# Silu as one activation, and weight loads issued apart from their conversion, in a gated-attention kernel with a feed-forward block

## The chip, the cores and the metric

The kernel runs on one core of one Trainium2 chip. The metric is the device time of one execution in microseconds (us); lower is better. A profile is one traced execution, whose span is a little shorter than the time. The engines are PE (TensorE, matrix products), PEld (its weight loads), DVE (VectorE), ACT (ScalarE), POOL (GpSimd) and SP (SyncE, here only an issuer of DMAs). The granted clock is the share of PE's full clock that the profile's records show.

Unless a range is given, times are medians. The executions of one kernel spread over 0.4 to 4.7 us (the kernel before over 7.1 us in eleven executions), so a difference under 2 us between two times is not resolved; where one matters, I read it from the traces. The experiments ran on two chips, on which the kernel before took much the same (medians of 736.81 and of 737.04 to 737.39), and each ratio is to the kernel before in the same rounds.

## The reference, cut to what matters

```python
# attention: a complex-valued decaying state per head, over 768 steps
mag = np.sqrt(a_re*a_re + a_im*a_im)
scale = np.minimum(mag, 0.999) / (mag + 1e-06)
...
S_re, S_im = ar*S_re - ai*S_im + kv, ar*S_im + ai*S_re
y[:, :, t] = einsum(q[:, :, t], S_re)
# feed-forward on the 3072 rows of y
h = x @ w_in                    # 384 -> 2048
g = h * (1.0 / (1.0 + np.exp(-h)))   # silu
return g @ w_out                # 2048 -> 384
```

Everything is float32 inside the kernel; the weights come as float64 and are converted on the chip by integer operations on DVE.

## The kernel before

The 768 steps are cut into chunks of 128; with 4 batches that makes 24 chunks, handled as 12 pairs. A pair goes through these stages:

1. gates: logarithm, exponential and arctangent on ACT, a phase sum on PE, sines on ACT;
2. rotation of k and q on DVE, transposition into `T` (on PE for early chunks; on DVE and by DMA for later ones);
3. attention scores `a`, state `s`, output `y` on PE, and a copy to `xT`;
4. hidden products `h` on PE, `g = silu(h)`, output products `o` on PE.

The hidden layer of one pair is interleaved with the attention of the next. The activation of a hidden group was made of two operations:

```python
def hidden(p, jp):
    ...                                     # 12 matmuls into ps: h, 128 x 512
    g = moe.tile([C, 2, T], F32, tag="g", name=f"g{p}_{jp}", bufs=4)
    special(g, ps, AF.Tanh, scale=0.5)                    # ACT
    with tc.high_priority():
        nc.vector.scalar_tensor_tensor(out=g, in0=g, scalar=1.0, in1=ps,
                                       op0=ALU.add, op1=ALU.mult)   # DVE
# and at the end of a pair: nc.scalar.mul(out=ot, in_=..., mul=0.5)
```

From the fourth pair on every engine's order is written by hand. One step reads (h and r are hidden and output groups on PE, A and B the two chunks of the pair):

```python
usual = ("c h h E kA qA L F h kB h tA G r qB r h tB r th h A X r h r aA pA sA yA h pB aB S r lA "
         "sB yB r lB D r")
# E: exp table, decays   L, F: logarithms, inverse   kA, qA: rotation   tA: transposes for T
# G: ratio, arctangent   aA: scores
```

Before that only PE's order is fixed; the other engines' order is chosen when the program is built. The start:

```python
load_a(0)                      # gate inputs of the first pair, by SP
load_a(1, g)                   # of the second pair, by POOL (g = nc.gpsimd)
gates(0, True)                 # squares, then the exp table, logarithms, ...
table("trig"); gates_atan(0, True); gates_square(1); gates_angle(0, True)
both(phases, 0); both(sums, 0); turns(0)
gates_log(1); gates_inverse(1); gates_ratio(1)
convert(3)                     # each: fetch a block of weights, then convert it
...                            # k, q, v of the first pair, by SP
```

## Time and profile before

| what | us |
|---|---|
| time, median (range of 4 runs) | 738.94 (737.51 to 739.36) |
| span of the profile | 737.3 |
| PE busy, DVE busy, ACT busy | 678.7, 392.2, 352.2 |
| first matmul (phases of the first pair) | 22.88 |
| first hidden matmul | 70.58 |
| first scores of the second hand-ordered step, where the regular steps begin | 287.91 |
| six steps from there | 332.50 (55.4 each) |

PE is nearly always busy after the first hidden matmul. So the table is read as a relay: how late PE gets its first real work, how long it takes from there to the regular part, and how long a regular step lasts. An engine's busy total says little by itself. The lines of the profile stand in the prediction below.

### The profile page before, as it was taken

Reading aid. Unit: us, or ns where it says so; the run is one execution under the profiler, and the core shown is the slowest. Engines: PE = TensorE matmul, PEld = TensorE weight load, DVE = VectorE, ACT = ScalarE, POOL = GpSimd, SP = SyncE. Lnnn points to the kernel's source line nnn. Section 1 sums busy time; section 2 is a strip of 40 time slices with the busy share of each in tenths; the row PEclk is TensorE's granted clock in tenths of the full one; section 3 lists DMA queues with packets and bytes.
Section 4 is the critical chain, followed back from the end, with each engine's and each line's share of the span. In section 5 each row is a group of like instructions: output and inputs, shape, how many; then the busy total and the mean of one; then the engine's idle time right before and its main releaser. Section 6 shows DMA issues by size and latency. Waiting matters only on the chain.

```text
span 737.3 us, 9570 instructions
## 1 busy us (share of the span) xinstructions
PE 678.7 (92%) x3552; PEld 513.2 (70%) x3552; DVE 392.2 (53%) x638; ACT 352.2 (48%) x589; POOL 72.1 (10%) x111
## 2 busy tenths in 40 slices
PE   0465999899999999999999999999999999999997
PEld 0154877568667777777777777777777777778774
DVE  3878889835463348348348348348348347262110
ACT  6987569367572461461461461461461461331201
POOL 2355021030110010010010010010010010010000
PEclk9986999999999999999999999999999999999999
DMA  9494654010160005605605604605605605414000
GB/s 188 112 233 123 159 146 144 22 43 2 49 108 1 20 8 79 138 6 85 125 12 79 132 10 76 134 13 81 128 12 79 131 11 80 99 19 68 29 1 25
DMA packets 205894, 55.52 MB, mean 75 GB/s; under 512 B 196376, under 2 KB 200624, under 8 KB 205840
## 3 DMA queue, kind: packets, MB, share of 16 engines
q1 hardware_dynamic: 198096, 43.05, 30.3%
q0 software_dynamic: 4288, 7.06, 4.6%
q10 hardware_dynamic: 3456, 4.72, 1.7%
q8 instruction: 30, 0.49, 0.3%
q14 instruction: 24, 0.20, 0.1%
HBM read 36.25 MB, written 4.76 MB: 56 GB/s over the span
## 4 chain that ended last, share of the span: by engine, by line
PE 64%; ACT 11%; DVE 9%; SPq 5%; issue 5%; DMA 4%; POOL 1%; DVEq 0%; ACTq 0%; POOLq 0%
PE o L472 23%; PE h L457 22%; PE a L390 5%; SPq L382 5%; PE s L439 4%; PE y L411 3%; ACT s L227 3%; ACT mag L227 2%; PE y L414 2%; PE L L327 2%; ACT L222 2%; DMA raw<-in_moe_w_in_dram 2%; DVE g L462 2%; PE phase L306 2%; DMA T<-sq 1%
## 5 line engine op out<-in xcount | busy, mean ns | idle before, releaser
L457 PE MATMUL h<-xT,w 128*128 128x256 f32 x1152 | 261.7, 382 | 7.9 <-DMA decs<-ends 7.9
L472 PE MATMUL o<-w,g 128*128 128x384 f32 x768 | 262.8, 490 | 0.0
L457 PEld LDWEIGHTS h<-xT,w 128*128 128x128 f32 x1152 | 219.6, 192 | 49.7 <-ACT x L181 8.1
L472 PEld LDWEIGHTS o<-w,g 128*128 128x128 f32 x768 | 145.0, 191 | 89.8 <-issue 3.7
L462 DVE SCALAR_TENSOR_TENSOR g<-g,h 128x512 f32<-128x512 f32 x96 | 65.1, 683 | 202.0 <-ACT g L227 201.8
L227 ACT ACTIVATE g<-h 128x512 f32<-128x512 f32 x96 | 55.3, 594 | 153.8 <-PE h L457 153.6
L341 POOL DMA_DIRECT2D decs<-ends x48 | 30.1, 634 | 443.8 <-DMA ends<-eq 443.5
L420 ACT COPY xT<-y 128x384 f32<-128x384 f32 x24 | 11.5, 478 | 120.0 <-PE y L414 109.4
L390 PEld LDWEIGHTS a<-T 96*128 96x128 f32 x384 | 46.4, 194 | 14.1 <-issue 8.4
L390 PE MATMUL a<-T 96*128 96x128 f32 x384 | 48.3, 279 | 5.2 <-DMA T<-sq 3.0
L222 ACT ACT_TABLE_LOAD x41 | 52.6, 1283 | 0.7
L227 ACT ACTIVATE mag<-mag 128x768 f32<-128x768 f32 (+1 forms) x39 | 30.5, 788 | 44.9 <-DVE mag L272 44.5
L306 PE MATMUL phase<-th,upto 128*128 128x384 f32 x48 | 21.5, 549 | 25.6 <-DVE th L285 25.2
L330 DVE TENSOR_SCALAR L<-L 128x384 f32<-128x384 f32 x24 | 13.3, 556 | 54.6 <-PE L L327 54.6
L395 DVE TENSOR_TENSOR w<-a,upto 128x512 f32<-128x512 f32 x48 | 32.0, 684 | 18.2 <-PE a L390 18.2
L411 PE MATMUL y<-w,v 128*64 128x128 f32 (+1 forms) x384 | 39.6, 281 | 0.0
L414 PE MATMUL y<-T,S 96*64 96x128 f32 x320 | 34.2, 273 | 0.0
L439 PEld LDWEIGHTS s<-v,kr 128*96 128x96 f32 x320 | 29.9, 165 | 5.8 <-issue 2.2
L478 ACT ACTIVATE ot<-o 128x384 f32<-128x384 f32 x24 | 11.8, 490 | 40.3 <-PE o L472 40.3
L439 PE MATMUL s<-v,kr 128*96 128x48 f32 x320 | 30.0, 247 | 0.9 <-DVE w L395 0.8
L227 ACT ACTIVATE s<-s 128x768 f32<-128x768 f32 (+1 forms) x39 | 30.5, 784 | 0.3
L306 PEld LDWEIGHTS phase<-th,upto 128*128 128x128 f32 x48 | 9.0, 207 | 28.6 <-issue 26.3
(71 smaller groups left out, 648.4 us busy)
## 6 DMA issues: line engine op xcount, KB each, us to landing
T<-sq SPq DMA_DIRECT2D x192, 64.0 KB
raw<-in_moe_w_out_dram SPq DMA_DIRECT2D x16, 384.0 KB
raw<-in_moe_w_in_dram SPq DMA_DIRECT2D x24, 192.0 KB
out_dram<-ot ACTq DMA_DIRECT2D x24, 192.0 KB
k<-in_k_dram SPq DMA_DIRECT2D x18, 192.0 KB
q<-in_q_dram SPq DMA_DIRECT2D x18, 192.0 KB
v<-in_v_dram SPq DMA_DIRECT2D x18, 192.0 KB
re<-in_a_re_dram SPq DMA_DIRECT2D x16, 192.0 KB
```

The lines of the kernel that those rows point to most:

```text
L222: chain(nc.scalar.preload_act_table_set({"exp": "natural_log_exp_and_others", "trig": "trig_and_small", "atan": "sigmoid_and_others", "sin ...
L227: chain(nc.scalar.activation(out=out, in_=in_, func=func, **kw))
L306: nc.tensor.matmul(ps, lhsT=upto, rhs=th, start=True, stop=True)
L382: nc.sync.dma_start(out=to[ts(b, Q), :, a], in_=sq[ts(a, Q), b])
L390: nc.tensor.matmul(ps[:, h], lhsT=x["kT"][:, hh * HH + h], rhs=x["qT"][:, hh * HH + h], start=True, stop=True)
L395: nc.vector.tensor_tensor(out=x["w", hh], in0=ps, in1=upto.unsqueeze(1).to_broadcast([C, HH, C]), op=ALU.mult)
L411: nc.tensor.matmul(to, lhsT=v_[:, cols], rhs=x["w", h // HH][:, h % HH], start=True, stop=not carried)
L414: nc.tensor.matmul(to, lhsT=x["S"].rearrange("p h d -> p (h d)")[:, cols], rhs=x["qT"][:, h], start=False, stop=True)
L439: nc.tensor.matmul(ps[:, h], lhsT=x["kr"][:, h].rearrange("p c d -> p (c d)"), rhs=x["v"][:, h], start=True, stop=True)
L457: nc.tensor.matmul(ps[:, ji], lhsT=w1[:, dc, ts(jp * 2 + ji, C)], rhs=A[p]["xT"][:, dc], start=(dc == 0), stop=(dc == ND - 1))
L462: nc.vector.scalar_tensor_tensor(out=g, in0=g, scalar=1.0, in1=ps, op0=ALU.add, op1=ALU.mult)
L472: nc.tensor.matmul(A[p]["o"][m], lhsT=A[p]["g", jp][:, ji, ts(m, C)], rhs=w2[:, j], start=(j == 0), stop=(j == NJ - 1))
```

## The change

Silu becomes one ACT function, which frees DVE of 96 operations. Tanh and the arctangent ran from one table set; the kernel runs silu and the arctangent from two, so the arctangent now has a table load on each side; the separate load for the sines goes. The fetch of a weight block is split from its conversion, so that fetches can be issued early and in a chosen order with the gate inputs. The first table is loaded before the first inputs are there. The early transfers of `xT` go from POOL to SP.

```diff
-        special(g, ps, AF.Tanh, scale=0.5)
-        with tc.high_priority():
-            nc.vector.scalar_tensor_tensor(out=g, in0=g, scalar=1.0, in1=ps, op0=ALU.add,
-                                           op1=ALU.mult)
+        special(g, ps, AF.Silu)
...
-                nc.scalar.mul(out=ot, in_=A[p]["o"][m], mul=0.5)
+                nc.scalar.copy(out=ot, in_=A[p]["o"][m])
...
-            what["S"] = lambda: (table("sin"), both(trig, p + 1))
+            what["S"] = lambda: both(trig, p + 1)
-            what["F"] = lambda: (gates_inverse(p + 1), table("atan"))
-            what["G"] = lambda: (gates_ratio(p + 1), gates_atan(p + 1))
+            what["F"] = lambda: (gates_inverse(p + 1), table("silu"))
+            what["G"] = lambda: (gates_ratio(p + 1), table("trig"), gates_atan(p + 1),
+                                 table("silu"))
...                                   (the same for the early pairs)
-                (nc.sync if late else nc.gpsimd).dma_start(      # xT
+                nc.sync.dma_start(
...
-        load_a(1, g)
-        gates(0, True)
+        load_a(0)                     # one piece now on ACT's queue
+        fetch(2)
+        load_a(1)
+        fetch(1)
+        both(lambda n: load_x(n, "k"), 0)
+        both(lambda n: load_x(n, "q"), 0)
+        fetch(1)
+        both(lambda n: load_x(n, "v", g), 0)
+        table("exp")
+        gates_square(0, True)
...
```

Cut: the splitting of `load_w` into `fetch` and `convert` with four raw buffers in place of five, a sixth gate buffer, and the removal of pools that nothing used.

More of the change, by code (lines that the diff above doesn't have):

```diff
@@ L94 @@
     LB = 2
+    RAW = 4
     consts = ctx.enter_context(tc.tile_pool(name="consts", bufs=1))
@@ L133, in load_a @@
             for name, ap in (("re", a_re), ("im", a_im)):
-                (queue or nc.sync).dma_start(
+                (queue or (nc.scalar if p + i == 0 and name == "im" else nc.sync)).dma_start(
                     out=cut(A[p][name], i).rearrange("p (h d) -> p h d", d=D),
@@ L146, in load_x @@
                 out=X[n][name], in_=ap[b].rearrange("h (c p) d -> p c h d", p=C)[:, c])
-    units = []
     tiny = consts.tile([C, ND * (DF // WC) + NJ], F32)
@@ L152 @@
     w2 = consts.tile([C, NJ, DM], F32)
-    def load_w1(cols, dc):
-        load_w(w1[:, dc, ts(cols, WC)],
-               [(at, w_in[r:r + n, ts(cols, WC)]) for at, r, n in rows_in(H, D, ND, dc)])
-    def load_w2(j):
-        load_w(w2[:, j], [(0, w_out[ts(j, C)])])
-    def load_w(dst, parts):
-        n = dst.shape[1]
-        if parts[0][1].dtype == F32:
-            for at, src in parts:
-                nc.sync.dma_start(out=dst[at:at + src.shape[0]], in_=src)
-            return
-        raw = su.tile([C, WC, 2], I32, tag="raw", name="raw", bufs=5)[:, 0:n]
-        for at, src in parts:
-            nc.sync.dma_start(out=raw[at:at + src.shape[0]],
-                              in_=src.bitcast(I32).rearrange("p (n two) -> p n two", two=2))
-        lo, hi = raw[:, :, 0].bitcast(U32), raw[:, :, 1]
-        u = su.tile([C, WC], I32, tag="wu", name="u", bufs=2)[:, 0:n]
-        joined(nc, dst, lo, hi, u)
-        x = su.tile([C, WC], F32, tag="wx", name="x", bufs=1)[:, 0:n]
-        nc.scalar.activation(out=x, in_=hi.bitcast(F32), func=AF.Square, scale=2.0 ** 15)
-        nc.scalar.activation(out=x, in_=x, func=AF.Relu, scale=-1.0, bias=least_b,
-                             accum_out=tiny[:, ds(len(units), 1)])
-        units.append(dst)
@@ new lines, with fetch @@
+    blocks = []
+    for s in range(DF // WC):
+        for dc in range(ND):
+            blocks.append((w1[:, dc, ts(s, WC)], (1, s), [
+                (at, w_in[r:r + n, ts(s, WC)]) for at, r, n in rows_in(H, D, ND, dc)]))
+        for j in range(s * WC // C, (s + 1) * WC // C):
+            blocks.append((w2[:, j], (2, j // 2), [(0, w_out[ts(j, C)])]))
+    fetched, done = [], []
+    def fetch(n):
+        for dst, _, parts in blocks[len(fetched):len(fetched) + n]:
+            raw = su.tile([C, WC, 2], I32, tag="raw", name="raw", bufs=RAW)[:, 0:dst.shape[1]]
+            for at, src in parts:
+                if src.dtype == F32:
+                    nc.sync.dma_start(out=dst[at:at + src.shape[0]], in_=src)
+                else:
+                    nc.sync.dma_start(
+                        out=raw[at:at + src.shape[0]],
+                        in_=src.bitcast(I32).rearrange("p (n two) -> p n two", two=2))
+            fetched.append(raw)
@@ new lines, in convert @@
+    def convert(n):
+        for dst, _, parts in blocks[len(done):len(done) + n]:
+            if len(done) == len(fetched):
+                fetch(1)
+            raw = fetched[len(done)]
+            done.append(dst)
+            if parts[0][1].dtype == F32:
+                continue
+            lo, hi = raw[:, :, 0].bitcast(U32), raw[:, :, 1]
+            u = su.tile([C, WC], I32, tag="wu", name="u", bufs=2)[:, 0:dst.shape[1]]
+            joined(nc, dst, lo, hi, u)
+            x = su.tile([C, WC], F32, tag="wx", name="x", bufs=1)[:, 0:dst.shape[1]]
+            nc.scalar.activation(out=x, in_=hi.bitcast(F32), func=AF.Square, scale=2.0 ** 15)
+            nc.scalar.activation(out=x, in_=x, func=AF.Relu, scale=-1.0, bias=least_b,
+                                 accum_out=tiny[:, ds(len(done) - 1, 1)])
@@ L187, in keep, with converted @@
+    def converted(which):
+        while any(x[1] == which for x in blocks[len(done):]):
+            convert(1)
     def keep(t, pattern, base, mult, fill=0.0):
@@ L222, in table @@
         chain(nc.scalar.preload_act_table_set({
-            "exp": "natural_log_exp_and_others", "trig": "trig_and_small", "atan": "sigmoid_and_others",
-            "sin": "silu_and_others"}[of]))
+            "exp": "natural_log_exp_and_others", "trig": "trig_and_small",
+            "silu": "silu_and_others"}[of]))
     def special(out, in_, func, **kw):
@@ L240, in gates_square @@
         for x in ("s1", "s2", "mag"):
-            g[x] = flat(pre.tile([C, 2, H, D], F32, tag="t3", name=f"{x}{p}", bufs=5))
+            g[x] = flat(pre.tile([C, 2, H, D], F32, tag="t3", name=f"{x}{p}", bufs=6))
         for x in ("l", "th"):
@@ L316, in trig @@
         x = X[n]
-        x["cs"] = pre.tile([C, H, 2, D], F32, tag="t3", name=f"cs{n}", bufs=5)
+        x["cs"] = pre.tile([C, H, 2, D], F32, tag="t3", name=f"cs{n}", bufs=6)
         special(x["cs"][:, :, 1], heads(x["turn"]), AF.Sin, scale=TWO_PI)
@@ L427, in output @@
             for dc in range(ND):
-                (nc.sync if late else nc.gpsimd).dma_start(
+                nc.sync.dma_start(
                     out=xT[64 * r + D:64 * r + 64, dc],
@@ L512, in step @@
         else:
-            what["F"] = lambda: table("atan")
+            what["F"] = lambda: table("silu")
         if p + 2 < NP:
@@ L523, in part @@
             if f is hidden:
-                converted(1, jp // 2)
+                converted((1, jp // 2))
             else:
-                converted(2, jp)
+                converted((2, jp))
             f(p, jp)
@@ L535, in parts @@
         return take
-    load_a(0)
-    conv = []
-    for s in range(4):
-        conv += [(1, s, lambda s=s, dc=dc: load_w1(s, dc)) for dc in range(ND)]
-        conv += [(2, j // 2, lambda j=j: load_w2(j)) for j in range(4 * s, 4 * s + 4)]
-    def converted(which, i):
-        while any(x[:2] == (which, i) for x in conv):
-            conv.pop(0)[2]()
-    def convert(n):
-        for _ in range(n):
-            if conv:
-                conv.pop(0)[2]()
     def attend(n):
@@ L589 @@
     with tc.manual_schedule(engines={mybir.EngineType.PE}):
-        load_a(1, g)
-        gates(0, True)
+        load_a(0)
[4 more added lines that the diff above has]
+        both(lambda n: load_x(n, "q"), 0)
+        fetch(1)
+        both(lambda n: load_x(n, "v", g), 0)
+        table("exp")
+        gates_square(0, True)
+        gates_log(0, True)
+        gates_inverse(0, True)
+        gates_ratio(0, True)
         table("trig")
@@ L602 @@
         convert(3)
-        both(lambda n: load_x(n, "k"), 0)
-        both(lambda n: load_x(n, "q"), 0)
-        both(lambda n: load_x(n, "v"), 0)
         for n in (0, 1):
@@ L616 @@
         turns(1)
-        table("sin")
+        table("silu")
         for n in (2, 3):
@@ L632 @@
         gates(2)
-        table("atan")
+        table("silu")
         convert(7)
         groups("r0 r0 r1 r1 h1 h1")
+        table("trig")
         angles(2)
+        table("silu")
         groups("h0 h0")
@@ L642 @@
         groups("r1 r1 h1 h1")
-        table("sin")
         turns(2)
-        table("sin")
+        table("silu")
         for n in (4, 5):
@@ L655 @@
         attend(5)
-        table("atan")
+        table("trig")
         angles(3)
+        table("silu")
         groups("r0 r0 r1 r1")
@@ L661 @@
         load_a(4, g)
-        table("sin")
         both(trig, 3)
@@ L666 @@
         late.append(fast.enter_context(tc.tile_pool(name="late", bufs=1)))
-        late.append(fast.enter_context(tc.tile_pool(name="o_late", bufs=2, space=PSUM)))
-        late.append(fast.enter_context(tc.tile_pool(name="h_late", bufs=1, space=PSUM)))
-        late.append(fast.enter_context(tc.tile_pool(name="m_late", bufs=1, space=PSUM)))
         late.append(fast.enter_context(tc.tile_pool(name="o_late", bufs=2, space=PSUM)))
```

## The prediction

> **What bounds the kernel now.** I read the page first: its busy shares and slices, then the stretches, then the tensor engine's own timeline with the idle time ahead of each group, and last ACT and DVE in the two places where that timeline shows idle time.
>
> ```profile
> PE 678.7 (92%) x3552; PEld 513.2 (70%) x3552; DVE 392.2 (53%) x638; ACT 352.2 (48%) x589; POOL 72.1 (10%) x111
> PE   0465999899999999999999999999999999999997
> PEclk9986999999999999999999999999999999999999
> ```
>
> PE is busy 92% of the span, and its idle time lies in the first four slices (74 us). The clock is low only in the third and fourth.
>
> ```profile
> 60.00:80.00 20.00, 12.00 (x73) 10.40 (x74) 16.47 (x32) 12.33 (x27) 10.14 (x15) 0.74 0.48 137
> 80.00:100.00 20.00, 19.56 (x146) 16.18 (x145) 18.40 (x39) 8.67 (x20) 5.06 (x8) 1.00 0.65 165
> 311.60:367.40 55.80, 54.75 (x297) 41.87 (x297) 29.28 (x43) 24.25 (x38) 2.50 (x4) 1.00 0.40 73
> ```
>
> The columns are stretch and length, then busy time of PE, weight loads, DVE, ACT and POOL, granted clock, DMA share, GB/s. From 80 us on PE is full. In a repeated step of some 55 us DVE is busy 29 and ACT 24: relieving them buys nothing by itself. So the time is (start of the first hidden-layer matmul) + (a nearly solid PE queue), plus a few gaps.
>
> ```profile
> 22.88 2.90 PE L306 MATMUL phase<-th,upto 128*128 128x384 f32 x4 [22.88 <-DVE th L285]
> 51.17 2.68 PE L306 MATMUL phase<-th,upto 128*128 128x384 f32 x4 [2.36 <-DVE th L285]
> 61.63 1.09 PE L411 MATMUL y<-w,v 128*64 128x128 f32 x16
> 70.58 7.75 PE L457 MATMUL h<-xT,w 128*128 128x256 f32 x24 [7.86 <-DMA decs<-ends]
> ...
> 343.68 2.02 PE L390 MATMUL a<-T 96*128 96x128 f32 x16 [1.05 <-DMA T<-sq]
> ```
>
> The first matmul waits 22.9 us for the first pair's angles; the dense part starts at 70.58, after the transposed attention result xT has been moved. Later the only recurring gap is before the attention scores: 0.42, 1.05, 0.37, 0.52, 0.18, 0.37, 0.62 and 0.84 us over the steps, together 4.4.
>
> The front is an ACT chain:
>
> ```profile
> 7.08 0.52 ACT L227 ACTIVATE s<-re 128x384 f32<-128x384 f32 x1 [1.52 <-DMA re<-in_a_re_dram]
> 8.87 0.52 ACT L227 ACTIVATE s<-im 128x384 f32<-128x384 f32 x1 [1.27 <-DMA im<-in_a_im_dram]
> 9.30 0.51 ACT L227 ACTIVATE th<-re 128x384 f32<-128x384 f32 x1
> 9.83 1.28 ACT L222 ACT_TABLE_LOAD   x1
> 11.12 0.52 ACT L227 ACTIVATE s<-s 128x384 f32<-128x384 f32 x1
> ```
>
> ACT waits for gate inputs until 8.87, loads a table on the path, and only then takes logarithms. From 12 to 24 us it is busy 11.75 of 12.
>
> **What the Trainium skill says.**
> 1. "ScalarE: Activation LUTs", What ACT_TABLE_LOAD costs: a load takes about 1283 ns whatever the set. The trace agrees (41 loads, mean 1283). It adds about 1380 ns of drain; here the function after a load starts at once (9.83+1.28, next at 11.12), so I count 1.28.
> 2. Same page, What happens when an `exp` ACTIVATE runs: one element per cycle per lane for every function. The trace holds tanh of 128x512 at 594 ns; so I take silu at 594 too. No run has shown silu yet.
> 3. "DMA: Bandwidth & Descriptors", Queues, rings and completion order: each DMA engine takes turns between queues at packet granularity. In the trace the second pair's loads, issued by POOL from 1.78 us, are in flight with the first pair's on SP; the first pair's last piece, issued at 2.80, reached ACT only at 8.87, six us later, against 2.9 for its first piece (0.82 to 3.69).
> 4. "TensorE: Matmul & The Clock Gate", Part 1: the clock is halved when PE has been idle and comes back after sustained work. The trace agrees: the first 24 hidden matmuls took 7.75 us at 70.58, later ones 5.34.
>
> **The change part by part.**
>
> *Silu for tanh and a product.* 96 DVE operations of 683 ns go: 65.1 us, so DVE busy should fall to about 327. ACT keeps 96 operations of the same length; the final scaling becomes a copy of the same length. Table loads: silu and arctangent do not share a set, so the arctangent now has a load before and one after. I count the calls: before 14 early and 27 in the steps, and one set by the compiler, 42; after 15 early, and in the steps 9 exp, 10 silu and 8 pairs around the arctangent, 35: in all 50. Eight more are 10.3 us of ACT work, busy about 362.
>
> What is on the path? In a step DVE stands behind the product of g:
>
> ```profile
> 267.63 0.95 DVE L263 TENSOR_TENSOR mag<-mag,th 128x768 f32<-128x768 f32 x1
> 273.37 0.69 DVE L462 SCALAR_TENSOR_TENSOR g<-g,h 128x512 f32<-128x512 f32 x1 [4.79 <-ACT g L227]
> 273.98 0.55 DVE L350 TENSOR_TENSOR L<-k,L 128x384 f32<-128x384 f32 x1
> ...
> 276.04 0.97 DVE L377 STREAM_TRANSPOSE sq<-kr 128x768 f32<-128x768 f32 x1
> 279.49 0.55 DVE L350 TENSOR_TENSOR eq<-q,eq 128x384 f32<-128x384 f32 x1
> ```
>
> It idles 4.79 us for ACT, though the operations behind it (k's rotation, then the transposes that feed T's transfers) are ready. Without the product it goes on at 268.6, and the first transpose starts near 268.6 + 0.55 + 0.88 = 270.0, not 276.04. T is then some 5 to 6 us earlier, and PE's wait for it, at most 1.05 us, is gone. Worth: the 4.4 us listed, taken as 4.
>
> *Start-up loads.* The gate inputs of the first pair no longer share the DMA engines with the second pair's, and one piece is issued by ACT's queue. They are 4 x 192 KB = 0.79 MB; at about 210 GB/s (mean of 193, 220 and 240 in 4-us stretches from 4 to 16 us) that is 3.7 us, after a first landing at some 2.9: the last lands near 6.2 in place of 8.8. That takes 2.6 us from the chain. The exp table is now loaded first, while the inputs travel: 1.28 off the path. Less other changes of order (one conversion in between, 0.5 us), I take 4.5 us for the first phase matmul, 22.9 to about 18.4. The same ACT/DVE work lies between it and the first hidden matmul, so that moves by the same 4.5.
>
> *Transfer of xT by SP and not POOL.* ACT has finished both copies of y at 63.42; POOL was at another issue until 63.91, then needed 6 x 0.487 = 2.92 us of issue, and h began at 70.58. SP needs 6 x 0.587 = 3.5 us in later steps, but without the 0.49 of waiting and with a free POOL. I take 1 us.
>
> *Weights fetched apart from conversion, five raw buffers to four; sixth gate buffer; pools removed.* Conversion runs 13 us or more ahead of its use (blocks of the third quarter converted by 107, first used near 122), so none of it is on the path after 70 us; zero. Duplicate pools were never used: zero.
>
> Sum: 4.5 + 1 + 4 + 0.5 (two small waits for copies of T before 225 us, 1.7 and 0.3, of which I give a quarter) = 10.0. 738.9 - 10.0 = 728.9 us.
>
> **The rivals.**
>
> *Early weight fetches delay the second pair's gates.* By the end of the second pair's inputs 0.79 + 1.05 (two raw blocks) + 0.79 = 2.6 MB must have come: at 210 GB/s 12.5 us, from about 2.5: 15 us. ACT will want them near 21.5 - 4.5 = 17. It speaks against this that there is 2 us to spare, for it that the engines are at a 0.99 share over the first 20 us. If it holds, 2 to 4 us of the gain are lost: 731 to 733.
>
> *SP becomes a blocked queue.* SP issues in order, and before the change stood 48.3 us in all, up to 8.0 at once, at raw fetches whose buffer DVE still had. If the xT transfers come to lie behind one of these (and now with four buffers), the dense part starts up to 8 us later than I say: about 733 to 737.
>
> *ACT becomes the bound inside a step.* The arctangent now brings 2.57 us of loads. Against: ACT waited 5.78 us for DVE's ratio before the arctangent at 279.61, and with DVE freed that ratio comes some 6 us earlier. The next g was done at 281.7 and is wanted by PE at 284.75. If I am wrong, PE waits for g, 1 to 2 us in each of 8 steps: 729 becomes 737 to 745.
>
> *The start gains more.* Idle ACT or DVE time between 23 and 70 us could close as well, since conversions interleave differently. There are 58.6 us of PE idle in all, most of it here; another 5 us would make it 723.
>
> **Range and chances.** The sum is 728.9; I say 729. The rivals that cost are each less likely than not and reach 737; the one that gains reaches 722. So 722 to 736. Two per cent is 14.8 us, a time under 724.1: it takes my whole sum and 5 us of the front besides, 0.18. Slower by 2% would need 754: only a broken overlap could do it, 0.02. Within: 0.80.
>
> **What would show it.** Right: first phase matmul near 18.4, first hidden matmul near 65, last-minus-first of the dense part shorter by 4; DVE busy 327, ACT 362, 50 table loads, silu near 594 ns; no PE wait for T in the steps; first transpose of a step before g is wanted. Wrong: the second pair's squares waiting on DMA, an SP wait on raw buffers just before xT, PE waiting on ACT for g in each step, or a first hidden matmul still near 70.

## The result, and the profile after

The changed kernel took 721.75 us (721.14 to 723.45, 4 runs) against 738.94: ratio 0.9774, 95% interval 0.9753 to 0.9796. Ratios here are the mean time of one kernel's runs over that of the other's of the same rounds, so not quite the ratio of the medians. Run again later, five rounds gave 723.65 (721.18 to 723.81) and 0.9804 (0.9777 to 0.9831). The gain is 14 to 17 us, about 2.1%; the predicted 729.0 was 10. The 721.75 lies a quarter of a us below the range that I gave, and "faster by over 2%", true of the first measurement, had a chance of 0.18.

The page, as before (busy shares, then slices of 18 us):

```profile
PE 673.2 (93%) x3552; PEld 512.2 (71%) x3552; DVE 334.3 (46%) x542; ACT 362.8 (50%) x597; POOL 59.7 (8%) x91
PE   0486997999999999999999999999999999999997
PEclk9998999999999999999999999999999999999999
```

DVE lost 57.9 us, not the 65.1 that its 96 operations add up to: back-to-back operations overlap (two masks of w of 0.684 us each took 1.28 us in a row at 59.40 in the kernel before), so removing one of a row saves less than its duration. ACT is at 362.8 with 50 table loads, as worked out. PE's busy time fell by 5.5 us although it does the same 3552 matmuls. Of this 2.4 us lie between the first matmul and the first hidden one, where the granted clock rose from 0.87 to 0.97; 1.7 lie in the six regular steps, where it was 1.00 in both kernels and only the overlap of matmuls differs, as told below.

PE's timeline at the points that the prediction showed (start, duration, idle time ahead and what ended it in brackets):

```profile
19.45 2.90 PE L322 MATMUL phase<-th,upto 128*128 128x384 f32 x4 [19.45 <-DVE th L301]
46.34 1.73 PE L322 MATMUL phase<-th,upto 128*128 128x384 f32 x4
54.41 1.09 PE L427 MATMUL y<-w,v 128*64 128x128 f32 x16
61.75 7.54 PE L473 MATMUL h<-xT,w 128*128 128x256 f32 x24 [6.25 <-DMA xT<-y]
...
120.64 2.93 PE L322 MATMUL phase<-th,upto 128*128 128x384 f32 x4 [2.55 <-DVE th L309]
124.68 1.56 PE L343 MATMUL L<-l,half 128*128 128x384 f32 x4 [1.11 <-DVE turn L326]
```

The first matmul is 3.4 us earlier, the first hidden one 8.8. The second pair's phases no longer wait and take 1.73 us in place of 2.68. At 120.64 there is a larger wait than before: at the same point, the third pair's phases, PE had waited 0.34 us and then 2.11.

ACT at the start, answering to the lines in the prediction:

```profile
5.56 0.52 ACT L243 ACTIVATE s<-re 128x384 f32<-128x384 f32 x1
7.40 0.52 ACT L243 ACTIVATE s<-im 128x384 f32<-128x384 f32 x1 [1.32 <-DMA im<-in_a_im_dram]
7.83 0.51 ACT L243 ACTIVATE th<-re 128x384 f32<-128x384 f32 x1
8.24 0.51 ACT L243 ACTIVATE s<-s 128x384 f32<-128x384 f32 x1
```

The first logarithm starts at 8.24 (11.12 before), straight after the last square, with no table load between.

DVE in a regular step:

```profile
257.05 0.95 DVE L279 TENSOR_TENSOR mag<-mag,th 128x768 f32<-128x768 f32 x1
257.92 0.55 DVE L366 TENSOR_TENSOR L<-k,L 128x384 f32<-128x384 f32 x1
258.51 0.96 DVE L370 TENSOR_TENSOR kr<-L,cs 128x768 f32<-128x768 f32 x1
259.38 0.97 DVE L393 STREAM_TRANSPOSE sq<-kr 128x768 f32<-128x768 f32 x1
```

The wait of 4.79 us for ACT is gone. The exp table load that opens the step was at 251.72 here and at 262.30 before, so the first transpose comes 7.66 us into the step in place of 13.74 (the prediction's 270.0 would have been 7.7).

And what that does on PE, first the kernel before, then the changed one, at the same step:

```profile
616.82 2.74 PE L472 MATMUL o<-w,g 128*128 128x384 f32 x8
620.41 2.02 PE L390 MATMUL a<-T 96*128 96x128 f32 x16 [0.84 <-issue]
```

```profile
601.01 2.74 PE L485 MATMUL o<-w,g 128*128 128x384 f32 x8
603.59 1.95 PE L406 MATMUL a<-T 96*128 96x128 f32 x16
```

From one start to the next it is 3.59 us before and 2.58 after: the gap cost 1.01, though the column of idle time says 0.84. Matmuls are pipelined; after a gap the next one cannot start in the tail of the last (0.17 us here), and it runs 0.07 longer.

Where the 16.9 us between the two spans lie:

| stretch | before | after | difference |
|---|---|---|---|
| to the first matmul | 22.88 | 19.45 | -3.4 |
| from there to the first hidden matmul | 47.70 | 42.30 | -5.4 |
| from there to the first scores of the regular steps | 217.33 | 215.00 | -2.3 |
| six regular steps | 332.50 | 326.84 | -5.7 |
| the rest | 116.89 | 116.81 | -0.1 |

### The profile page after: what moved, and what is told of

Read it like the earlier page. It is cut to its first block, busy times and chain, and to the rows that moved or that the text cites.

```text
span 720.4 us, 9485 instructions
## 1 busy us (share of the span) xinstructions
PE 673.2 (93%) x3552; PEld 512.2 (71%) x3552; DVE 334.3 (46%) x542; ACT 362.8 (50%) x597; POOL 59.7 (8%) x91
## 4 chain that ended last, share of the span: by engine, by line
PE 86%; ACT 5%; DVE 3%; DMA 3%; SPq 2%; issue 1%; ACTq 0%
PE h L473 33%; PE o L485 32%; PE a L406 6%; PE s L455 4%; PE y L427 3%; PE y L430 2%; PE phase L322 2%; PE L L343 2%; PE tp L386 2%; DMA raw<-in_moe_w_in_dram 1%; ACT s L243 1%; ACT L238 1%; DMA q<-in_q_dram 1%; ACT mag L243 1%; SPq L135 1%
## 5 line engine op out<-in xcount | busy, mean ns | idle before, releaser
L238 ACT ACT_TABLE_LOAD x50 | 64.2, 1283 | 2.2 <-PEq L840 1.3
L366 DVE TENSOR_TENSOR L<-k,L 128x384 f32<-128x384 f32 x24 | 13.3, 554 | 82.2 <-ACT L L243 82.2
L324 DVE TENSOR_SCALAR turn<-phase 128x384 f32<-128x384 f32 x24 | 13.3, 556 | 42.3 <-PE phase L322 42.3
L491 ACT COPY ot<-o 128x384 f32<-128x384 f32 x24 | 11.5, 478 | 40.4 <-PE o L485 40.4
```

Source lines behind the costliest of these rows:

```text
L238: chain(nc.scalar.preload_act_table_set({"exp": "natural_log_exp_and_others", "trig": "trig_and_small", "silu": "silu_and_others"}[of]))
```

## The experiments

My theory after the comparison: two separate gains, the start (loads and queues) for the front and silu for the steps, the latter because of DVE's place in the order. The rivals were that loads and queues do it all, or that it is DVE's amount of work that counts, or that what follows the loads makes the front shorter. All kernels gave correct results.

### Silu alone

The kernel before, with the first parts of the diff above (silu, copy, table loads), loads and queues untouched.

> The kernel before with the silu part alone (silu for tanh and product, its table loads, copy for the last scaling); loads and queues as before. Theory (two separate gains): the step of 55.1 to 55.8 us between attention scores becomes 54.5 as in the changed kernel, since DVE no longer stands behind the product; the first hidden matmul stays near 70.6; time about 731 to 732. Rival (the steps are shorter because SP's queue was rearranged): steps stay above 55, time 738 to 739.

Measured: 724.09 us (722.44 to 726.65), ratio 0.9804 (0.9768 to 0.9841): 14.5 us, twice what I expected of it. The six steps take 326.83 us, as in the changed kernel, and the first hidden matmul comes at 69.05. The theory of the steps holds and the rival (SP's queue) falls. But half of the gain lies elsewhere: the stretch from the first hidden matmul to the regular steps is 212.45 us, 4.9 shorter (1.7 of it a stretch of low clock in the profile before, told of below). The first matmul came at 23.99, 1.1 us later than before, though the loads are the same: ahead of the fourth pair the order outside PE is chosen anew at every build, so no run here changes one thing alone in the front.

### The start alone, with the new table loads

```diff
-        special(g, ps, AF.Silu)
+        special(g, ps, AF.Tanh, scale=0.5)
+        with tc.high_priority():
+            nc.vector.scalar_tensor_tensor(out=g, in0=g, scalar=1.0, in1=ps, op0=ALU.add,
+                                           op1=ALU.mult)
```

This is on the changed kernel, with the final factor 0.5 back; all loads, queues and table loads stay.

> The changed kernel with tanh and the DVE product back in the old place, all loads and queues and table loads as changed. Theory: first hidden matmul near 61.8, steps back to 55.1 to 55.8 with a wait for T before the scores, time about 728. Rival (loads carry everything): time stays at 722. Other rival (silu is what shortens the front as well): first hidden matmul at 66 or later, time above 732.

Measured: 736.12 us (735.11 to 736.41), ratio 0.9972 (0.9940 to 1.0004): nearly nothing left. The first hidden matmul is at 61.03 and the six steps are back at 332.78, both as the theory said. But the middle takes 223.47 us, 6.1 longer than before: of the 9.5 us won at the front, 3.4 remain where the regular steps begin. One place where it is lost, ACT ahead of copies of `T`:

```profile
205.64 1.08 ACT L243 ACTIVATE g<-h 128x512 f32<-128x512 f32 x2
206.74 1.28 ACT L238 ACT_TABLE_LOAD   x1
210.79 0.84 ACT L243 ACTIVATE mag<-mag 128x768 f32<-128x768 f32 x1 [2.77 <-DVE mag L288]
211.65 1.28 ACT L238 ACT_TABLE_LOAD   x1
212.95 0.60 ACT L243 ACTIVATE g<-h 128x512 f32<-128x512 f32 x1
213.44 1.06 ACT L389 COPY T<-tp 96x512 f32<-96x512 f32 x2
```

ACT stands in order behind an arctangent that waits for DVE, which still has the products, and then behind the table load that brings the tanh back. PE waits 3.14 us for the copies; it waited 1.71 before, and 0.39 in the changed kernel. The other place is the wait at the third pair's phases, 3.31 us, followed by slow matmuls.

### The start alone, with the old table loads

The kernel of the last run, with tanh and arctangent in one set again and no loads around the arctangent: the other half of the change by itself.

```diff
-            what["F"] = lambda: (gates_inverse(p + 1), table("silu"))
-            what["G"] = lambda: (gates_ratio(p + 1), table("trig"), gates_atan(p + 1),
-                                 table("silu"))
+            what["F"] = lambda: (gates_inverse(p + 1), table("atan"))
+            what["G"] = lambda: (gates_ratio(p + 1), gates_atan(p + 1))
```

> The kernel before with the loads, queues and early exp table of the changed one, and its own table scheme (tanh together with arctangent, no loads around the arctangent). The run with the new scheme kept only 3 of its 9.5 us of front gain, losing them at the third pair's phases and at copies of T that stood behind two table loads on ACT. Theory (the extra loads, with the product still on DVE, give the front's gain back): first hidden matmul near 61, the wait at the third pair's phases under 1.5 us, at the copies of T under 2, time 729 to 732. Rival (the front's gain is lost because the rest cannot follow, whatever the tables): 735 to 737.

Measured: 728.30 us (727.51 to 728.67), ratio 0.9878 (0.9850 to 0.9905): 9 us. PE's waits:

```profile
PE h L473 <- DMA xT<-y: 6.1, 1, 6.1
...
PE a L406 <- DMA T<-sq: 3.1, 6, 0.7
PE tp L386 <- ACT T L389: 2.6, 5, 1.7
...
PE phase L322 <- DVE th L309: 1.8, 2, 1.6
```

The columns are the total, the number of waits and the longest. The longest wait for copies of `T` is 1.7 and the longest at the third pair's phases 1.6, both half of the last run's and the latter 0.1 above what I had written. So the extra table loads, as long as DVE still makes the products, cost 7 to 8 us (by the ratios 0.9972 and 0.9878, and by 736.12 against 728.30) and give most of the start's gain back. In the traces 7.5 of it lies in the middle (215.98 us here, 223.47 in the last run) and 0.8 in the six steps (331.99, 332.78). The rival falls.

Together, by the ratios: the start alone is worth 9 us, silu with its table loads 14.5, both 14 to 17. They are not additive: some 7 to 9 us of their sum are missing. In the traces the middle stretch is shortened 1.4 by the start and 4.9 by silu, but only 2.3 by both.

### The product in another place of DVE's order

If the place in DVE's queue is the cause in the steps, a kernel with all of the products should have short steps once they stand behind the transposes. On the run with tanh and product and new tables, the products of the third and fourth group of a step are held back:

```diff
+        if by_hand and jp in (2, 3):
+            waiting.append(product)
...
-                what["t" + x] = lambda n=n: turned(n)
+                what["t" + x] = lambda n=n: (turned(n), flush())
```

> As the run with tanh and product back, but in the hand-ordered steps the products of the third and fourth hidden group are issued behind the first transposes on DVE, ahead of their use. DVE does just as much work, about 393 to 400 us. Theory (it is the place in DVE's in-order queue, not DVE's work): steps about 54.5, no wait for T, time 6 us below the run with the product in the old place, about 722. Rival (DVE's 65 us of work are the cause): steps as with the product in its old place, time about 728.

Measured: 739.04 us (737.41 to 739.62), ratio 1.0007. A miss on the time: two single waits had come in, at steps whose order differs:

```profile
PE o L502 <- DVE g L480: 10.2, 2, 8.2
```

Yet its six steps, 290.45 to 617.29, took 326.84 us. I limited the edit to the regular steps (`3 <= p <= NP - 2` in the condition) and ran it again.

> The run with tanh and product in which the product stands behind the transposes, now only in the repeated steps: in the earlier form two single waits of PE for g, 8.2 us in the first hand-ordered step and 2.0 us in the last, hid the effect. Theory (place in DVE's queue): steps 54.5 us, no wait for T, DVE busy about 394 as with the product in its old place, time 5 to 7 us below that run, about 730. Rival (DVE's amount of work): steps 55.3 on average, time 736.

Measured: 728.78 us (725.54 to 730.26), ratio 0.9895 (0.9865 to 0.9924), 6 to 7 us below the same kernel with the product in its old place (736.12 and 0.9972, in other rounds). DVE in a step, and the scores on PE:

```profile
262.99 0.97 DVE L394 STREAM_TRANSPOSE sq<-kr 128x768 f32<-128x768 f32 x1
263.88 0.94 DVE L394 STREAM_TRANSPOSE sq<-qr 128x768 f32<-128x768 f32 x1
266.40 1.29 DVE L480 SCALAR_TENSOR_TENSOR g<-g,h 128x512 f32<-128x512 f32 x2 [1.58 <-ACT g L244]
```

```profile
277.78 2.74 PE L502 MATMUL o<-w,g 128*128 128x384 f32 x8
280.36 1.95 PE L407 MATMUL a<-T 96*128 96x128 f32 x16
```

DVE is busy 394.7 us, as much as with tanh before, and the distance on PE is 2.58 us, the same as with silu; the six steps take 326.84. So in the steps silu's gain is not the 58 us of DVE work at all. It is that an in-order engine no longer stands waiting for ACT with ready work behind it. The rival (amount of work) falls.

### The old order of loads

The changed kernel with the loads of the start as they were (the piece on ACT's queue goes back to SP, too):

```diff
-        fetch(2)
-        load_a(1)
-        fetch(1)
-        ...
+        load_a(1, g)
         table("exp")
...
         convert(3)
+        both(lambda n: load_x(n, "k"), 0)      # likewise q, v
```

> The changed kernel with the loads at the start as they were: second pair's gate inputs from POOL at once, no early weight fetches, k, q and v after the first conversions, all of the first pair on SP; silu, the early exp table and xT on SP stay. Theory (the front's gain is mostly the order of loads): first phase matmul back by 2 to 3 us (near 22), first hidden matmul near 65 to 67, time 725 to 727. Rival (the front's gain comes from what follows the loads, the second pair's gates being finished before attention starts): first phase 22 but first hidden matmul near 62 to 63, time 722 to 723.

Measured: first matmul at 22.81, first hidden matmul at 66.70, so the order of loads accounts for the 3.4 us to the first matmul and for 4.9 of the 8.8 us to the first hidden one; the first theory's positions hold, the rival's 62 to 63 does not. The time is 723.99 (723.14 to 726.95), ratio 0.9807 (0.9776 to 0.9837): 0.3 to 2.2 us above the changed kernel's two medians and below the 725 to 727 that I expected. In the profiled execution, the slowest of the four, the regular steps begin at 281.43, 4.7 us later than in the changed kernel's first profile and 2.9 later than in its second. How much of the 4.9 us remains at the end in most executions is open within this spread.

### The exp table behind the squares

One line: `table("exp")` moved below the first `gates_square`.

> The changed kernel with the first exp table load behind the squares, so that a table is loaded on the way as before. Theory: first phase matmul 1.3 us later, all later by as much, about 723.0. Rival (the inputs' arrival covers it): 721.7.

Measured: first matmul at 21.63 (2.2 us later, I had said 1.3), first hidden matmul 2.5 us later; 725.37 us (722.55 to 726.77), ratio 0.9843 (0.9816 to 0.9870). Of the 2.2 us, 1.36 are the load (the first logarithm starts at 9.60 in place of 8.24); most of the rest is that the order chosen at the build had put more of a weight conversion among ACT's gate operations (from that logarithm to the ones behind the next table load it takes 9.84 us in place of 9.01). So at the front the rival (the inputs' arrival covers the load) falls. In the time it is less clear: the medians are 1.7 and 3.6 us above the changed kernel's two, and the interval of the ratio overlaps with that of its second measurement. The profiled execution was the fastest of six, and at the regular steps it is only 0.5 us behind the changed kernel: no slow stretch followed its wait at the third pair's phases (the closing list has the clocks).

### xT by POOL

```diff
-                nc.sync.dma_start(
+                (nc.sync if late else nc.gpsimd).dma_start(
                     out=xT[64 * r + D:64 * r + 64, dc],
```

> The changed kernel with the early transfers of xT back on POOL's queue. Theory: the gap from the end of y to the first hidden matmul goes from 6.25 back to about 7.9 us, time 1.6 us longer, about 723.4. Rival (SP and POOL do it equally): 721.7.

Measured: 720.48 us (719.34 to 721.98), ratio 0.9776 (0.9749 to 0.9804): no slower. PE's waits:

```profile
PE h L473 <- DMA xT<-y: 7.6, 1, 7.6
...
PE phase L322 <- DVE th L309: 1.3, 1, 1.3
```

The gap at the first hidden matmul is 7.60 us (6.25 with SP), so the local part of the theory is right. The 1.3 us do not reach the end: PE comes to the third pair's phases 0.85 us later and waits there 1.28 in place of 2.55 us. That is no rule: in the runs with the late exp table and with the old loads PE came 1.8 and 4.7 us later and waited as long (2.57 and 2.56), since the angles came later as well.

### The second pair's gates ahead of all weights

In the start: `load_a(1)`, then `fetch(3)`.

> The changed kernel with the second pair's gate inputs ahead of all weight fetches. Rival of the prediction (early weights delay the second pair's gates): the second pair's squares, at 20.34 us in the changed kernel, come earlier and the first hidden matmul too, time 719 to 720. Theory (squares wait for ACT's place in the order, not for inputs): within 1 us of 721.7, or later, as the first conversion gets its block later.

Measured: 723.93 us (723.84 to 724.25), ratio 0.9822. The second pair's squares started at 17.75 in place of 20.34, but k's product with its decay came on DVE at 33.56 in place of 29.13: the order chosen when the program is built had put a weight conversion and a gate operation ahead of it. PE waited 9.73 us for the rotated k (5.54 in the changed kernel), and the first hidden matmul came at 64.94. The edit changed two things, so this run is inconclusive on the rival. It shows that an earlier input is worth nothing where another operation's place in the order sets the path. In the changed kernel itself ACT has no idle time ahead of these squares, so the sign that I had named (squares waiting on DMA) is not there; but SP issued the last two of their four inputs only at 13.02 and 15.40, so at the 17 us that I had worked out they would hardly have been there (in the kernel before, the first piece took 2.9 us from issue to use).

### The third pair's phases later in PE's order

If the wait at 120.64 is where gains are lost, PE should be given other work there:

```diff
-        groups("h0 h0")
+        groups("h0 h0 r1 r1")
         both(phases, 2)
         both(sums, 2)
...
-        groups("r1 r1 h1 h1")
+        groups("h1 h1")
```

> The changed kernel with the third pair's phase and decay matmuls put behind two result groups (5.2 us of PE work) in PE's order. In the changed kernel PE waits 2.55 and 1.11 us there and runs at the lower clock after it. Theory: these waits and the slow stretch go, 4 to 5 us, time about 717. Rival (the following conversions or decays then come late, and a wait opens after it): 720 to 722.

Measured: 718.17 us (717.53 to 719.66), ratio 0.9743 (0.9707 to 0.9779). The phases start without a wait. Part of the rival's wait is there, though: the decay sums behind them wait 1.07 and 0.62 us. From the first hidden matmul to the regular steps it takes 212.60 us, 2.4 less than in the changed kernel. The two were not run in the same rounds, and their ratios' intervals overlap with the first measurement of the changed kernel, so the gain rests on the trace.

### A version that beats both

The same, with one result group between phases and sums, and with the first transposes of the second pair ahead of the first hidden group, in the time in which PE waits for `xT`:

```diff
+        turned(2)
         groups("h0 h0")
...
-        groups("h0 h0")
+        groups("h0 h0 r1")
         both(phases, 2)
+        groups("r1")
         both(sums, 2)
```

> The changed kernel with three shifts in PE's order: one result group ahead of the third pair's phases and one between these and the decay sums, and the first transposes of the second pair ahead of the first hidden group, in the 6 us in which PE waits for xT. Theory: 4 to 5 us at the phases and 1 to 2 at the front, about 716. Rival (the transposes wait for their own input and push the first hidden group back): 718 to 719, no better than the run with the phases alone.

> The changed kernel as it is, for a comparison on the same chip in the same rounds. Both theories: 721 to 723.

Measured in the same rounds: 714.04 us (713.71 to 715.89), ratio 0.9698 (0.9673 to 0.9722), against 723.65 for the changed kernel (0.9804). That is more than I expected.

```profile
61.77 6.34 PE L473 MATMUL h<-xT,w 128*128 128x256 f32 x24
...
117.51 1.45 PE L322 MATMUL phase<-th,upto 128*128 128x384 f32 x4
118.80 2.74 PE L485 MATMUL o<-w,g 128*128 128x384 f32 x8
121.38 1.90 PE L343 MATMUL L<-l,half 128*128 128x384 f32 x4
```

No group has a bracket: there is no wait left here. The first hidden group starts no later for the transposes put before it and takes 6.34 us in place of 7.54 (8.44 in the second profile of the changed kernel).

## Why the prediction was right or wrong

**The start of the front: mechanism right, 4.5 us predicted, 3.4 measured.** The 4.5 was a wrong sum: its terms, 2.6 + 1.28 - 0.5, make 3.4. That this is what was measured is luck, for the terms were off. Inputs came sooner, but the last piece of the first pair reached ACT at 7.40 in place of 8.87, 1.5 us and not 2.6 (by its own terms "near 6.2" should have read 2.9 + 3.7 = 6.6, and the mean of the three rates is 218 GB/s, not 210). The table load left the path: from that piece to the first logarithm it takes 0.84 us in place of 2.25, so 1.4. From there to the first matmul it takes 11.21 in place of 11.76, half a us gained where I had put half a us lost. The runs with the old loads (22.81) and with the late table (21.63) each give most of it back; the two overlap, so their parts cannot be added.

**The step that failed.** "The same ACT/DVE work lies between it and the first hidden matmul, so that moves by the same 4.5." With 1 us for `xT` I had 5.5; it moved by 8.8. The work between the first matmul and the first hidden one was not the same length: 5.4 us went there. Of these, 1.4 lie before the second pair's phases and 1.6 at the transfer of `xT` (1 predicted). The other 2.4 are PE's own: from the second phases to the state products it took 3.79 + 2.72 + 2.46 us from start to start before and 2.84 + 1.56 + 2.18 after. Columns as in the prediction, first the kernel before, then the changed one:

```profile
51.00:57.00 6.00, 4.72 (x7) 2.15 (x8) 4.09 (x10) 4.96 (x13) 1.80 (x2) 0.53 1.03 205
```

```profile
46.00:51.00 5.00, 3.88 (x18) 1.69 (x15) 4.58 (x10) 4.32 (x11) 2.76 (x3) 1.00 0.53 134
```

The granted clock (third number from the right) was 0.53 in that stretch and is now 1.00. This goes with the wait of 2.36 us ahead of it: the three profiled executions with such a wait (2.36 before, 2.35 with silu alone, 1.91 with the old loads) have clocks of 0.52, 0.75 and 0.54 in the 6 us from the start of the second phases, and the eleven without one have 1.00. I had cited the clock gate and then counted all work of the front as fixed in length.

**The regular steps: mechanism right, 4 predicted, 5.7 measured over six steps.** The term was summed from the idle column: seven of the eight gaps lie within the six steps, 3.95 us. That column misses the lost overlap and the slower first matmuls, 0.17 and 0.07 us at the gap shown above; seven times 0.24 is the missing 1.7. The place of the product in DVE's order is shown as the cause by the run that keeps the product and moves it.

**The middle: 0.5 predicted, 2.3 measured, and its mechanism only half seen.** I expected the waits for copies of `T` to shrink by a quarter; the longest went from 1.71 to 0.39. I did not foresee two things. One is a longer wait at the third pair's phases, where the arctangent's table load now lies on the path:

```profile
115.19 1.28 ACT L238 ACT_TABLE_LOAD   x1
116.49 0.84 ACT L243 ACTIVATE mag<-mag 128x768 f32<-128x768 f32 x1
117.36 0.96 DVE L299 SCALAR_TENSOR_TENSOR mag<-re,mag 128x768 f32<-128x768 f32 x1 [1.54 <-ACT mag L243]
```

PE waits 2.55 us for the angles in place of 0.34, but 1.11 in place of 2.11 for the decay sums behind them, so 1.2 us of the front's gain are lost there. The load alone does not do it: with silu alone it lies on the path as well, and PE waits 0.92 and 1.11; in the changed kernel PE also comes there 7.7 us earlier. The other is the clock: in the profiled execution before, PE ran from 133 to 140 us at a clock of 0.76, which made one result stretch 1.7 us longer than after. That is not a property of either kernel: in the second profile of the changed kernel it is the changed kernel that has a slow stretch there.

**The rivals.** "Early weight fetches delay the second pair's gates" could not be told cleanly: its sign did not appear, but the run made for it changed two things. "SP becomes a blocked queue" did not happen: `xT` was issued at 56.22, at once after the copy that ended at 56.20. "ACT becomes the bound inside a step" did not happen in the steps, but its mechanism, the added loads around the arctangent, appeared one stage earlier, and cost 7 to 8 us when the product stayed on DVE. "The start gains more" did happen: 3.3 us over my 5.5 at the first hidden matmul.

**The attribution, beyond the number.** My sum gave the start 5.5 us and silu 4 to 4.5. By experiment silu with its tables is worth 14.5 alone and the start 9 alone. Most of the 10 that I predicted came from reading single waits one at a time; what the parts do together at the third pair's phases was not in it. Open remains how much of the front's gain survives in a typical execution, since the clock there changes from run to run.

## What to carry to other kernels

Look for ready work that stands behind a waiting operation on an in-order engine: moving or removing that one operation can shorten the path even where the engine is half idle, and counting its busy time does not show it. A gain at the front must be followed through the next point where several engines meet; here some of it became a longer wait at the third pair's phases until PE was given other work there. When PE idles for a few us, count not only the gap but also the lost overlap and a possible stretch at half the clock.

## What the Trainium skill lacked or had wrong

- "TensorE: Matmul & The Clock Gate", Part 1 and HAM oscillation, ties the slow clock to idle windows of some 3.4 us and warns of gaps longer than that. Here a gap of 2.36 us (kernel before) was followed by a clock of 0.53 over the next 6 us, and the 8 us around a gap of 2.55 us (changed kernel) had 0.79, while in the run with the late exp table the 8 us around a gap of 2.57 us at the same point had 1.00, and so had the 14 us around a gap of 3.31 us (product behind the transposes, regular steps only). The page's free-running window fits this spread; its advice on gap length is too generous.
- "ScalarE: Activation LUTs", Table sets, names neither a set with silu nor one with sine and arctangent. Here silu and sine ran from one set, sine and arctangent from another, with correct results; 96 silus of 128x512 took 596 ns each, tanh 594, as the page's rule of one rate for all functions (Step-by-step: what each stage is for) says.
- The same page, What ACT_TABLE_LOAD costs, adds about 1380 ns of drain to the 1283 ns of a load. No run here shows it: in the kernel before the logarithm at 11.12 starts 1.29 us after the load at 9.83, and that load starts as soon as the operation ahead of it ends (9.30 + 0.51).
- The skill tells that back-to-back matmuls overlap, but no page says that the idle column of a profile leaves out what a gap takes from that overlap: 0.84 us in the column were 1.01 us from start to start.
